# Linear attention and a routed feed-forward: rows of h scattered by expert slot, statistics and gates per unit

## Chip, cores and metric

One core of one Trainium2 chip. The metric is the device time of one execution in microseconds (us); lower is better. Five engines run their own instruction streams and meet at semaphores: TensorE (PE in the profile; its weight loads are PEld), VectorE (DVE), ScalarE (ACT), GpSimd (POOL) and SyncE (SP), which here only issues transfers.

## The reference, cut to what matters

```python
def _A_ref(x, wqkv, w_phi, wo):              # S = 2048 rows, D = 512, 32 heads of 16
    q, k, v = ...
    pq = jnp.einsum("bhsd,hdf->bhsf", q, w_phi)
    pk = jnp.einsum("bhsd,hdf->bhsf", k, w_phi)
    phi_q = jnp.concatenate([_softmax(pq, axis=-1), _softmax(-pq, axis=-1)], axis=-1)
    phi_k = jnp.concatenate([_softmax(pk, axis=-1), _softmax(-pk, axis=-1)], axis=-1)
    kv = jnp.einsum("bhsf,bhsd->bhfd", phi_k, v)
    z  = jnp.einsum("bhsf->bhf", phi_k)
    num = jnp.einsum("bhqf,bhfd->bhqd", phi_q, kv)
    den = jnp.einsum("bhqf,bhf->bhq", phi_q, z)[..., None] + 1e-6
    return (num / den) ... @ wo

def _B_ref(x, w_gate, w1, w2):               # E = 8 experts, F = 1792, one expert a row
    logits = xf @ w_gate
    topk_idx = jnp.argsort(-logits, axis=-1)[:, :K]
    topk_val = jnp.take_along_axis(logits, topk_idx, axis=-1)
    gates = _softmax(topk_val, axis=-1)
    for e in range(E):
        w = (gates * (topk_idx == e)).sum(-1, keepdims=True)
        out = out + w * (_silu(xf @ w1[e]) @ w2[e])

h = x + _A_ref(_layernorm(x), ...)
h2 = h + _B_ref(_layernorm(h), ...)
```

Each row goes to the one expert with the largest logit. Everything is float32; the large products are computed as three products of a rounded high part and the remainder (`mm3`, lines 74 to 77).

## The kernel before, in words

The 2048 rows are 16 chunks of 128. The work has three stages.

**Features (lines 384 to 452).** For each chunk c the loop at line 409 loads x two chunks ahead on SyncE's queue (`s_ln`, `load_x`), normalises, transposes (`s_tr`), projects to k, v and q, and sums k-features times v over all chunks (`s_kv`, line 372). x has three buffers, its normalised form another three.

**Output and routing (lines 457 to 599).** For each chunk: numerator and denominator (`s_num`), transposes (`s_ot`), the output projection `po` (`s_wo`). `s_wo` adds x to make h, and computes h's mean and reciprocal deviation (bn_stats and aggregate on VectorE, two operations on GpSimd). h, these two and the gate are one row of 516 numbers in `hb`; two chunks are a batch, and `s_top` picks the expert of each row, computes the gate by powers on GpSimd, and sends the batch to a DRAM buffer `hbuf` in token order. `s_rank` counts each row's place within its expert by matmuls with triangular and all-ones matrices, and `s_inv` adds one-hot products into a table `ivf` that maps places to tokens. After eight chunks `s_star` takes the expert with the most rows so far as the first one; its weights `raw` are loaded, and `split_chunk` divides them into `whi` (ScalarE) and `wlo` (VectorE or, for 10 of the 16 quarter chunks, GpSimd), while the last chunks are still worked on. `s_first` gathers the first unit's rows; all four chunks of its gemm1 are computed in this stage, interleaved with the last output projections.

**Units (lines 601 to 807).** A unit is a block of 128 rows of one expert. `gather(u)` brings its rows from `hbuf` by an indirect transfer on GpSimd's queue, two units ahead. `prework` normalises and transposes them; `gemm1` (48 matmuls) goes through silu and transposes (`tr`, giving `hThi`, `hTlo`) to `gemm2` (`g2`, 42 matmuls into `my`), then `yo` is scattered to the output. Where the next unit has another expert, `split` divides new weights under a condition read from a table, chunks 4 to 6 in the unit itself and 0 to 3 in the unit before, and `fetch` loads the expert after it. ScalarE, VectorE and GpSimd all take part in these conditions. `tables` (line 639) computes the block tables inside unit 0, behind its transposes, and `index` turns places into token numbers with 22 comparisons against `ivf`.

The order of instructions on an engine is not the source order: the framework orders by readiness in its own estimate and by source position, so a later instruction whose inputs and buffers are there can be issued ahead. `issue_after` pins one behind another.

Of the kernel before, what the change touches and what calls it, by code (L numbers as in the profile page):

```python
# [21 lines left out]
P = 128  # L22
# [10 lines left out]
ROW = D + 4  # L33
# [8 lines left out]
def kernel(  # L42
# [17 lines left out]
    hbuf = dram.tile([S, ROW], F32, name="hbuf")  # L60
# [13 lines left out]
    def mm3(ps, ahi, alo, bhi, blo, first, last):  # L74
# [12 lines left out]
    iota128 = consts.tile([P, P], F32, name="iota128")  # L87
    G.iota(iota128, pattern=[[1, P]], base=0, channel_multiplier=0, allow_small_or_imprecise_dtypes=True)
    iotaS = consts.tile([P, NT], F32, name="iotaS")
    G.iota(iotaS, pattern=[[P, NT]], base=0, channel_multiplier=0, allow_small_or_imprecise_dtypes=True)  # L90
    tok1 = consts.tile([P, NT], F32, name="tok1")
    G.iota(tok1, pattern=[[P, NT]], base=1, channel_multiplier=1, allow_small_or_imprecise_dtypes=True)
# [11 lines left out]
                    pattern=[[1, EV], [-1, EV]], channel_multiplier=0)  # L104
    gidx = consts.tile([P, NU], I32, name="gidx")
    sidx = consts.tile([P, NU], I32, name="sidx")
    isnew = consts.tile([P, NU], I32, name="isnew")
# [3 lines left out]
    ivf = consts.tile([P, P], F32, name="ivf")  # L111
    cnt = consts.tile([P, E], F32, name="cnt")
    col = consts.tile([P, NU], F32, name="col")
    star = consts.tile([P, E], F32, name="star")
    est = consts.tile([P, 1], F32, name="est")
    esti = consts.tile([P, 1], I32, name="esti")
    ps = ctx.enter_context(tc.tile_pool(name="ps", bufs=4, space=PSUM))
# [19 lines left out]

    def gather(u):
        G.indirect_dma_start(out=xg[u % 3], out_offset=None, in_=hbuf if u else hbuf[0:S // 2, :],
                             in_offset=bass.IndirectOffsetOnAxis(ap=gidx[:, u:u + 1], axis=0))  # L140

    def prework(u):
        g = xg[u % 3]
        xi = V.tensor_scalar(xn2[0], g[:, 0:D], g[:, D:D + 1], g[:, D + 1:D + 2], op0=OP.subtract, op1=OP.mult)
        pt = bank("mtr")
        for k in range(KD):
            T.transpose(pt[:, k * P:(k + 1) * P], xn2[0][:, k * P:(k + 1) * P], ident)
        ptv = pt.rearrange("p (k t) -> p k t", k=KD)
        hi_of(xhi[u % 2], ptv)
        lo_of(xlo[u % 2], ptv, xhi[u % 2])  # L150
        return xi
# [16 lines left out]
    LO = (V,) * NW  # L168

    def split_chunk(c, lo=None, n=2):  # L170
        for i in range(n):
            w = slice(i * (CW // n), (i + 1) * (CW // n))
            hi_of(whi[c][:, w], raw[c][:, w])
            eng = lo or LO[c]
            eng = eng[i] if isinstance(eng, tuple) else eng
            eng.tensor_tensor(wlo[c][:, w], raw[c][:, w], whi[c][:, w].bitcast(F32), op=OP.subtract)  # L176
# [15 lines left out]
    with ExitStack() as actx:  # L192
# [11 lines left out]
        csg = keep.tile([P, 2, E // 2], F32, name="csg")  # L204
        xwg = keep.tile([P, NT, 2, E // 2], F32, name="xwg")
        kvbd = keep.tile([P, NG, 68], F32, name="kvbd")
        V.memset(kvbd, 0.0)
        cum = [keep.tile([P, E], BF16, name=f"cum{c}") for c in range(NT + 1)]
        V.memset(cum[0], 0.0)
        V.memset(ivf, 0.0)  # L210
# [50 lines left out]
        def s_num(c):  # L261
            load_x(c)
            o = row("o", 2, "pc").rearrange("p (h f) -> p h f", f=DH)
            for i in range(2):
# [6 lines left out]
                V.tensor_scalar(den, nv[:, :, DH:DH + 1], 1e-6, None, op0=OP.add)  # L271
                V.reciprocal(den, den)
# [9 lines left out]
        if True:  # L282
            wp = c1.enter_context(tc.tile_pool(name="wp", bufs=1))
            wgs = wp.tile([P, KD, E], F32, name="wgs")
            onesf = wp.tile([P, P], F32, name="onesf")
# [74 lines left out]
            def s_v(c):  # L360
# [4 lines left out]
                mc = work.tile([P, 2, E // 2], F32, name="mc")  # L365
                G.tensor_scalar(mc, csg, st[c]["mv"][:, 0:1], None, op0=OP.mult)
                G.tensor_tensor(xwg[:, c], xwg[:, c], mc, op=OP.add)
# [33 lines left out]
            V.tensor_copy(csg.rearrange("p i e -> p (i e)"), pc[:, 0:E])  # L401
# [4 lines left out]
            def s_q(c):  # L406
                st[c]["tq"] = feat1(proj(st[c]["x"], wqhi, wqlo, "pq"))

            for c in range(NT - 1):
# [7 lines left out]
                if c == 3:  # L417
                    pg = bank("pog")
                    for dt in range(KD):
                        for t in range(4):  # L420
                            T.matmul(pg[:, dt * E:(dt + 1) * E], woT_raw[t // 2][:, t % 2, dt * P:(dt + 1) * P],
                                     wgs[:, t, :], start=(t == 0), stop=(t == 3))
# [21 lines left out]
            for i in range(2):  # L444
                for h in range(4):
                    V.tensor_copy(kvbd[32 * h:32 * h + 32, 4 * i:4 * i + 4, 17 * h:17 * h + 17],
                                  kvps[i][32 * h:32 * h + 32, :, 17 * h:17 * h + 17])
# [9 lines left out]
        def s_wo(c):  # L457
            b, j = divmod(c, NB)
            po = proj2(st[c]["oT"], wohi, wolo, "po")
            if j == 0:  # L460
                bt[b]["hb"] = work.tile([P, NB * ROW], F32, name="hb", tag="ph", bufs=3).rearrange(
                    "p (j r) -> p j r", r=ROW)
                G.memset(bt[b]["hb"][:, :, D + 3:D + 4], 0.0)
                bt[b]["lg"] = work.tile([P, NB, E], F32, name="lg", bufs=3)
            h = bt[b]["hb"][:, j, :]
            V.tensor_tensor(h[:, 0:D].rearrange("p (i d) -> p i d", i=2), po[:, :, 0:D // 2],
# [3 lines left out]
            ln_rstd(h[:, 0:D], h[:, D:D + 2], h[:, D + 1:D + 2])  # L470
            V.scalar_tensor_tensor(lg, csg, h[:, D:D + 1], lg, op0=OP.mult, op1=OP.subtract)

        def s_top(b):
            hb, lg = bt[b]["hb"], bt[b]["lg"]
            mn = work.tile([P, NB, 1], F32, name="tmn")
            V.tensor_reduce(mn, lg, AX.X, OP.min)
            eq = work.tile([P, NB, E], F32, name="eq")
            V.tensor_tensor(eq, lg, mn.to_broadcast([P, NB, E]), op=OP.is_equal)
# [9 lines left out]
            gt = work.tile([P, 3, NB, 1], F32, name="gt")  # L488
            nr = work.tile([P, NB, 1], F32, name="nr")
            V.tensor_reduce(gt[:, 0], mn, AX.X, OP.min)  # L490
            G.tensor_tensor(gt[:, 0], gt[:, 0], mn, op=OP.subtract)
            G.tensor_tensor(gt[:, 0], gt[:, 0], hb[:, :, D + 1:D + 2], op=OP.mult)
            G.tensor_tensor(gt[:, 1], euler.to_broadcast([P, NB]).unsqueeze(2), gt[:, 0], op=OP.pow)
            G.tensor_scalar(gt[:, 2], gt[:, 1], 0.0, None, op0=OP.add)
            G.tensor_tensor(nr, gt[:, 2], mone.to_broadcast([P, NB]).unsqueeze(2), op=OP.pow)
            G.tensor_tensor(hb[:, :, D + 2:D + 3], gt[:, 1], nr, op=OP.mult)
            nc.sync.dma_start(hbuf[b * NB * P:(b + 1) * NB * P, :].rearrange("(c p) r -> p c r", p=P), hb)

        def s_rank(b):
# [8 lines left out]
            rk = work.tile([P, NB], F32, name="rk")  # L508
            V.tensor_reduce(rk, rs, AX.X, OP.add)
            bs = work.tile([P, NB], F32, name="rb")  # L510
            V.tensor_scalar(bs, rk, 0.25 - P / 2, FLOOR, op0=OP.add, op1=OP.add)
            V.tensor_scalar(bs, bs, FLOOR, None, op0=OP.subtract)
            sl = work.tile([P, NB], F32, name="sl")
            V.tensor_tensor(sl, rk, bs, op=OP.subtract)
            am = work.tile([P, NB, P], F16, name="am")
            bm = work.tile([P, NB, E, NT], F16, name="bm")
            for j in range(NB):
                c = b * NB + j
                V.tensor_scalar(am[:, j, :], iota128, sl[:, j:j + 1], None, op0=OP.is_equal)
                jm = work.tile([P, NT], F16, name="jm")  # L520
                V.tensor_scalar(jm, iotaS, bs[:, j:j + 1], tok1[:, c:c + 1], op0=OP.is_equal, op1=OP.mult)
                V.tensor_tensor(bm[:, j], bc(oh[:, j, :], NT), mid(jm, E), op=OP.mult)
# [331 lines left out]
```

## Time and profile before

| | |
|---|---|
| median of 3 runs (lowest to highest) | 733.07 us (732.66 to 734.25) |
| profiled execution, its own time | 732.92 us |
| its span | 731.2 us |
| TensorE busy, mean granted clock | 702.0 us (96%), 0.987 |
| VectorE, ScalarE, GpSimd busy | 468.8, 303.2, 180.8 us |
| features, output and routing, units | about 0 to 205, 205 to 317, 317 to 731 us |
| bytes moved | 87.61 MB, 9.21 MB of it written |

In rows of groups, `out<-in` names what is written and read, then shapes, the count, the busy time and the mean of one in ns, then the idle time of the engine just before and what ended it. In the timeline, a row has start and duration, and in brackets the idle time before it with the releaser. A DMA-issue row shows the issuing only.

### The profile page before, as it was taken

The numbers are of one execution on the slowest core, as the hardware profiler recorded it, in microseconds if no ns is written. First come the engines' busy times: TensorE is split into PE (matmuls) and PEld (weight loads), VectorE is DVE, ScalarE is ACT, GpSimd is POOL, SyncE is SP. The second block draws the span as 40 slices with busy tenths as digits, with TensorE's granted clock in tenths as the row PEclk, the third lists the DMA queues.
The fourth block names the chain that finished last, engine by engine and source line by source line (L and its number), as shares of the span: only waits on it lengthen the run. The fifth ranks groups of instructions, "written<-read, shape, count | busy, mean of one in ns | idle before, by whom it ended". The sixth has DMA issues, their size and how long they took to land.

```text
span 731.2 us, 12523 instructions
## 1 busy us (share of the span) xinstructions
PE 702.0 (96%) x4130; PEld 612.2 (84%) x4130; DVE 468.8 (64%) x969; ACT 303.2 (41%) x458; POOL 180.8 (25%) x281
## 2 busy tenths in 40 slices
PE   6999999999999998779999999999999999999996
PEld 6899999999989997658888888888888878888885
DVE  4996987878787889794512999972185472922211
ACT  4534444434322015152112888862274463822211
POOL 3364645434313328521110011110011111011110
PEclk9999999999999999899999999999999999999999
DMA  9111101100002249417400799981066381001000
GB/s 332 57 30 44 30 15 30 30 15 1 1 16 73 74 156 341 153 34 294 193 29 2 258 369 376 344 345 53 30 210 241 121 328 31 11 29 30 30 30 6
DMA packets 21912, 87.61 MB, mean 120 GB/s; under 512 B 3070, under 2 KB 3582, under 8 KB 14656
## 3 DMA queue, kind: packets, MB, share of 16 engines
q1 hardware_dynamic: 18624, 76.86, 28.8%
q0 software_dynamic: 3200, 9.75, 4.0%
q8 instruction: 34, 0.56, 0.3%
q14 instruction: 54, 0.44, 0.2%
HBM read 78.18 MB, written 9.21 MB: 120 GB/s over the span
## 4 chain that ended last, share of the span: by engine, by line
issue 46%; PE 35%; DMA 10%; DVE 6%; POOL 1%; ACT 1%; POOLq 1%; SPq 0%; DVEq 0%
DMA out_dram<-yo,sidx 8%; PE kvps L372 4%; PE pn L267 3%; PE pq L75 2%; PE pq L77 2%; PE pq L76 2%; PE ptq L381 2%; PE pv L77 2%; PE pv L76 2%; PE pv L75 2%; PE pk L75 2%; PE pk L77 2%; PE pk L76 2%; PE po L75 2%; PE po L76 2%
## 5 line engine op out<-in xcount | busy, mean ns | idle before, releaser
L69 ACT ACTIVATE whi<-raw 128x1024 fp32r<-128x1024 f32 (+1 forms) x120 | 118.7, 1003 | 67.9 <-PE mh L77 37.4
L176 DVE TENSOR_TENSOR wlo<-raw,whi 128x1024 fp32r<-128x1024 f32 (+1 forms) x110 | 130.6, 1200 | 18.6 <-ACT whi L69 12.5
L75 PE MATMUL mh<-whi,xhi 128*128 128x512 f32 (+1 forms) x304 | 114.9, 378 | 0.0
L77 PE MATMUL mh<-whi,xlo 128*128 128x512 f32 (+1 forms) x304 | 111.5, 367 | 0.0
L76 PE MATMUL mh<-wlo,xhi 128*128 128x512 f32 (+1 forms) x304 | 111.4, 366 | 0.0
L798 POOL DMA_INDIRECT out_dram<-yo,sidx x19 | 21.5, 1131 | 352.5 <-DVEq L635 202.0
L76 PE MATMUL my<-wlo,hThi 128*128 128x512 f32 x266 | 104.7, 393 | 3.5 <-DVE wlo L176 3.3
L75 PE MATMUL my<-whi,hThi 128*128 128x512 f32 x266 | 106.0, 399 | 0.3 <-ACT hThi L69 0.3
L77 PE MATMUL my<-whi,hTlo 128*128 128x512 f32 x266 | 104.6, 393 | 0.3 <-DVE hTlo L72 0.3
L72 DVE TENSOR_TENSOR hTlo<-mtr,hThi 128x512 fp32r<-128x512 f32 x76 | 47.0, 621 | 86.2 <-ACTq L635 53.3
L163 ACT ACTIVATE hs<-mh 128x512 f32<-128x512 f32 x76 | 41.0, 540 | 145.3 <-PE mh L77 145.3
L355 POOL TENSOR_TENSOR ph<-t,sm 128x1024 f32<-128x1024 f32 x32 | 62.1, 1939 | 66.9 <-DVE sm L353 37.8
L77 PEld LDWEIGHTS mh<-whi,xlo 128*128 128x128 f32 x304 | 57.2, 188 | 10.2
L76 PEld LDWEIGHTS mh<-wlo,xhi 128*128 128x128 f32 x304 | 57.3, 189 | 9.3
L75 PEld LDWEIGHTS mh<-whi,xhi 128*128 128x128 f32 x304 | 57.2, 188 | 9.3
L797 DVE SCALAR_TENSOR_TENSOR yo<-my,xg 128x512 f32<-128x512 f32 x19 | 14.2, 748 | 78.4 <-PE my L77 78.4
L76 PEld LDWEIGHTS my<-wlo,hThi 128*128 128x128 f32 x266 | 50.3, 189 | 14.2 <-DVE wlo L176 4.3
L77 PEld LDWEIGHTS my<-whi,hTlo 128*128 128x128 f32 x266 | 50.3, 189 | 11.2 <-DVE hTlo L72 0.5
L75 PEld LDWEIGHTS my<-whi,hThi 128*128 128x128 f32 x266 | 50.4, 189 | 10.5 <-ACT hThi L69 0.5
L352 DVE TENSOR_REDUCE sm<-t 128x64 f32<-128x1024 f32 x32 | 38.8, 1214 | 12.0 <-ACT t L347 11.9
L727 PE MATMUL mtr<-ident,hs 128*128 128x128 f32 x266 | 41.7, 274 | 2.7 <-DVE hTlo L72 2.6
L347 ACT ACTIVATE t<-t 128x1024 f32<-128x1024 f32 x32 | 33.9, 1061 | 20.9 <-DVE t L346 19.8
(206 smaller groups left out, 1407.3 us busy)
## 6 DMA issues: line engine op xcount, KB each, us to landing
raw<-in_w_dram SPq DMA_DIRECT2D x56, 1024.0 KB, 5.2
xt<-in_x_dram SPq DMA_DIRECT2D x32, 256.0 KB, 2.7
hbuf<-hb SPq DMA_DIRECT2D x8, 516.0 KB, 3.8
phT<-in_wqkT_dram SPq DMA_DIRECT2D x4, 512.0 KB, 5.1
phT<-in_wv_dram SPq DMA_DIRECT2D x2, 512.0 KB, 6.4
phT<-in_wo_dram SPq DMA_DIRECT2D x2, 512.0 KB, 8.2
phT<-in_woT_dram SPq DMA_DIRECT2D x2, 512.0 KB, 5.6
xg<-hbuf,gidx POOLq DMA_INDIRECT x21, 3.7
```

The source lines that it names most:

```text
L69: A.activation(dst, src, AF.Copy)
L72: V.tensor_tensor(dst, src, hi.bitcast(F32), op=OP.subtract)
L75: T.matmul(ps, ahi, bhi, start=first, stop=False)
L76: T.matmul(ps, ahi, blo, start=False, stop=False)
L77: T.matmul(ps, alo, bhi, start=False, stop=last)
L163: A.activation(hs[c % 2][:, 0:fw], p[:, 0:fw], AF.Silu)
L176: eng.tensor_tensor(wlo[c][:, w], raw[c][:, w], whi[c][:, w].bitcast(F32), op=OP.subtract)
L347: A.activation(t, t, AF.Exp)
L352: V.tensor_reduce(sm, t, AX.X, OP.add)
L355: G.tensor_tensor(ph.rearrange("p (a f) -> p a f", f=DH), t, bc(sm, DH), op=OP.mult)
L372: T.matmul(kvps[g // 4][:, g % 4, :], ph[:, g * P:(g + 1) * P], vt[:, 4 * g:4 * g + 4, :].rearrange("p h f -> p (h f)"), start=(c == 0 and ...
L727: T.transpose(pt[:, j * P:(j + 1) * P], hs[c % 2][:, j * P:(j + 1) * P], ident)
```

## The change

- `hbuf` has 8 x 2048 rows of 514 numbers: h, the largest logit, the token number. Each expert owns 2048 rows. `cum[0]` starts at 16 per partition and expert so that `s_rank`'s sum is the row's slot itself; `s_rank` then sends each chunk by an indirect scatter from GpSimd (`send`), 16 in all, in place of 8 plain stores on SyncE's queue. It moves to the head of the loop's iteration.
- Rows that no token fills must hold a token number that the output scatter drops, so `s_blank` writes one blank row to all of `hbuf`, in 14 transfers on SyncE's queue, one for each iteration of the feature loop.
- The one-hot products, `s_inv`, `ivf` and `index` go. A unit's row numbers are now base plus partition.
- Mean, deviation and gate are computed per unit, from the gathered rows (`stats`, `gating`). In `s_wo` the statistics go; the mean is removed from the logits by centred gate weights `wgc`, which also removes GpSimd's correction in `s_v`.
- The 1e-6 of the denominator is added once, in `kvbd`.
- All splits of the first expert's weights are on VectorE, two quarter chunks an iteration from c = 12; none is on GpSimd. GpSimd no longer takes part in the conditions.
- Of unit 0 one chunk of gemm1 is computed ahead of the tables, three behind them. `tables1` (row numbers) comes first in unit 0, with gathers 1 and 2 behind it; `tables2` (flags) comes after `tr(2)`. In later units `stats(u + 1)` stands behind the split of chunk 4, and `prework(u + 1)` behind `g2(0, 2)` and `tr(3)`.

```diff
-ROW = D + 4
+ROW = D + 2
-    hbuf = dram.tile([S, ROW], F32, name="hbuf")
+    hbuf = dram.tile([E * S, ROW], F32, name="hbuf")
...
+    def send(c, rows, hrow):
+        i = G.indirect_dma_start(out=hbuf, out_offset=bass.IndirectOffsetOnAxis(ap=rows, axis=0),
+                                 in_=hrow, in_offset=None)
+        for other in sent + fetched:
+            tc.declare_no_dep(i.ins, other.ins, reason="other rows of hbuf")
+        sent.append(i)
+
     def gather(u):
...
+        i = G.indirect_dma_start(out=xg[u % 3], out_offset=None, in_=hbuf,
+                                 in_offset=bass.IndirectOffsetOnAxis(ap=gidx[:, u:u + 1], axis=0))
+        for other in sent:
+            tc.add_manual_dep(i.ins, other.ins.name, mybir.DependencyInfo(
+                mybir.DependencyClass.Sync, mybir.DependencyReason.DATA), reason="rows of hbuf")
+        fetched.append(i)
+
+    def stats(u):
+        g = xg[u % 3]
+        bs = small.tile([P, 6], F32, name="ubs")
+        V.bn_stats(bs, g[:, 0:D])
+        V.bn_aggr(norm[:, u, :], bs)
+        ve = small.tile([P, 1], F32, name="uve")
+        G.tensor_scalar(ve, norm[:, u, 1:2], EPS, None, op0=OP.add)
+        G.tensor_tensor(norm[:, u, 1:2], ve, nhalf, op=OP.pow)
+        V.tensor_scalar(xn2[0], g[:, 0:D], norm[:, u, 0:1], norm[:, u, 1:2], op0=OP.subtract, op1=OP.mult)
+
+    def gating(u):
+        g = xg[u % 3]
+        sc = small.tile([P, 5], F32, name="usc")
+        V.tensor_reduce(sc[:, 0:1], g[:, D:D + 1], AX.X, OP.max)
+        G.tensor_copy(sidx[:, u:u + 1], g[:, D + 1:D + 2])
...
+        G.tensor_tensor(gate[:, u:u + 1], sc[:, 3:4], sc[:, 4:5], op=OP.mult)
...
     def prework(u):
-        g = xg[u % 3]
-        xi = V.tensor_scalar(xn2[0], g[:, 0:D], g[:, D:D + 1], g[:, D + 1:D + 2], op0=OP.subtract, op1=OP.mult)
         pt = bank("mtr")
...
-            eng.tensor_tensor(wlo[c][:, w], raw[c][:, w], whi[c][:, w].bitcast(F32), op=OP.subtract)
+            lo_of(wlo[c][:, w], raw[c][:, w], whi[c][:, w])
...
+            def s_blank(c):
+                n = E * S // (NT - 2) // P
+                lo, hi = c * n * P, min((c + 1) * n * P, E * S) if c < NT - 3 else E * S
+                n = (hi - lo) // P
+                nc.sync.dma_start(hbuf[lo:hi, :].rearrange("(p r) f -> p r f", p=P),
+                                  blank.to_broadcast([P, n, ROW]))
...
                 if c + 2 < NT:
                     s_ln(c + 2)
+                    s_blank(c)
...
-            ln_rstd(h[:, 0:D], h[:, D:D + 2], h[:, D + 1:D + 2])
-            V.scalar_tensor_tensor(lg, csg, h[:, D:D + 1], lg, op0=OP.mult, op1=OP.subtract)
...
-            nc.sync.dma_start(hbuf[b * NB * P:(b + 1) * NB * P, :].rearrange("(c p) r -> p c r", p=P), hb)
...
+            to = work.tile([P, NB], F32, name="to")
+            V.tensor_reduce(to, rs, AX.X, OP.add)
+            toi = slots[:, b * NB:(b + 1) * NB]
+            V.tensor_copy(toi, to)
+            G.tensor_copy(bt[b]["hb"][:, :, D + 1], tok[:, b * NB:(b + 1) * NB])
             for j in range(NB):
-                c = b * NB + j
-                V.tensor_scalar(am[:, j, :], iota128, sl[:, j:j + 1], None, op0=OP.is_equal)
-                jm = work.tile([P, NT], F16, name="jm")
-                V.tensor_scalar(jm, iotaS, bs[:, j:j + 1], tok1[:, c:c + 1], op0=OP.is_equal, op1=OP.mult)
-                V.tensor_tensor(bm[:, j], bc(oh[:, j, :], NT), mid(jm, E), op=OP.mult)
...
+                send(b * NB + j, toi[:, j:j + 1], bt[b]["hb"][:, j, :])
...
-        for c in range(NT + 8):
+        for c in range(NT + 2):
+            b, j = divmod(c - 3, NB)
+            if j == 0:
+                at(s_rank, b - 1, NT // NB)
...
-            if NT - 4 <= c < NT:
-                split_chunk(c - NT + 4, ((G, G, V, V), (G, G, G, V), (G, G, G, V), (G, G, V, V))[c - NT + 4], 4)
...
+            if c == NT + 1:
+                s_top(NT // NB - 1)
+            if NT - 4 <= c < NT + 2:
+                split_pieces(2)
+            if c == NT:
+                with tc.issue_after(st[NT - 3]["add"].ins):
+                    stats(0)
+            if c == NT + 1:
                 prework(0)
...
+        pre.append(gemm1(0, 0))
+        s_rank(NT // NB - 1)
+        split_pieces(len(pieces))
...
-                                                        engines=[ENG.Activation, ENG.DVE, ENG.Pool])
+                                                        engines=[ENG.Activation, ENG.DVE])
...
+        if u == 0:
+            tables1()
+            gather(1)
+            gather(2)
         g1(0)
         if u:
             split(u, 4)
+            if u + 1 < NU:
+                stats(u + 1)
+        else:
+            split_chunk(4)
         g1(1)
+        gating(u)
         tr(0)
         if u:
             split(u, 5)
+        else:
+            stats(1)
         g1(2)
         tr(1)
...
+            g2(py, 0, 4)
+            tr(3)
+            with tc.issue_after(held["gidx"].ins):
+                tables2()
...
+            g2(py, 4, 11)
+            prework(1)
+            g2(py, 11, 14)
...
+            g2(py, 0, 2)
+            tr(3)
+            if u + 1 < NU:
                 prework(u + 1)
```

More of the change, by code (lines that the diff above doesn't have):

```diff
@@ L719, in unit @@
+        V.tensor_tensor(le, mid(end, NU), bc(eend, EV), op=OP.is_le)
+        nx = rt.tile([P, NU], F32, name="nx")
+        V.tensor_reduce(nx, le, AX.X, OP.add)
+        V.tensor_scalar(nxt, nx, 1.0, float(E - 1), op0=OP.subtract, op1=OP.min)
+        V.scalar_tensor_tensor(more, nx, float(EV), nw, op0=OP.is_lt, op1=OP.mult)
     def unit(u):
@@ L755, in unit @@
             split(u, 6)
+        else:
+            split_chunk(5)
         g1(3)
```

244 lines of the change are left out of this document (91 added, 153 removed).

## Prediction

> **What bounds the kernel now.** I read the busy table and the 40 slices first, then ten-us windows, then the timeline inside the windows that stand out.
>
> ```profile
> PE 702.0 (96%) x4130; PEld 612.2 (84%) x4130; DVE 468.8 (64%) x969; ACT 303.2 (41%) x458; POOL 180.8 (25%) x281
> ```
>
> TensorE is busy for 702.0 of 731.2 us, so only its holes and its slow stretches can be won, unless its work shrinks. The windows (busy time of PE, PEld, DVE, ACT, POOL, then granted clock, DMA share, GB/s) show where they lie:
>
> ```profile
> 260.00:270.00 10.00, 10.00 (x94) 9.95 (x93) 7.82 (x42) 1.19 (x2) 3.10 (x8) 1.00 0.32 100
> 270.00:280.00 10.00, 8.03 (x71) 7.57 (x71) 8.22 (x39) 4.29 (x8) 4.92 (x9) 1.00 0.88 318
> 280.00:290.00 10.00, 8.80 (x55) 7.89 (x56) 10.00 (x30) 5.49 (x11) 9.58 (x13) 0.83 0.87 305
> 290.00:300.00 10.00, 5.56 (x37) 5.25 (x36) 10.00 (x34) 0.77 (x2) 9.07 (x15) 0.77 0.43 172
> 300.00:310.00 10.00, 10.00 (x65) 9.05 (x65) 5.65 (x25) 2.37 (x3) 3.19 (x8) 0.89 0.60 212
> 310.00:320.00 10.00, 9.67 (x59) 7.38 (x58) 8.86 (x45) 4.22 (x8) 3.23 (x8) 1.00 0.15 55
> 320.00:330.00 10.00, 6.26 (x24) 4.37 (x25) 9.76 (x34) 5.51 (x7) 2.16 (x2) 0.97 0.09 26
> 330.00:340.00 10.00, 10.00 (x41) 7.94 (x41) 6.08 (x16) 1.20 (x2) 2.00 (x2) 0.86 0.66 211
> ```
>
> From 260 to 270 us TensorE is full. Then it idles 1.97 + 1.20 + 4.44 us up to 300 and 0.33 + 3.74 us from 310 to 330, in sum 11.7 us. Its clock adds a loss: busy time times the missing share of the clock is 1.5, 1.3 and 1.1 us from 280 to 310 and 0.2 + 1.4 us from 320 to 340, in sum 5.5 us. So 17.2 us are lost between 270 and 340. VectorE is busy for all of 280 to 300, so it is what TensorE waits for. The timeline there:
>
> ```profile
> 279.93 0.77 PE L237 MATMUL pto<-ident,o 128*128 128x128 f32 x4 [1.97 <-DVE xl L72]
> 282.00:283.00 1.00, 1.00 (x7) 1.00 (x7) 1.00 (x10) 1.00 (x3) 0.83 (x3) 0.50 0.89 370
> 283.56 3.80 POOL L176 TENSOR_TENSOR wlo<-raw,whi 128x512 fp32r<-128x512 f32 x3
> 283.67 1.31 DVE L519 TENSOR_SCALAR am<-iota,sl 128x128 f16<-128x128 f32 x1
> 294.97 0.17 PE L504 MATMUL pl<-oh,tri 128*128 128x8 bf16 x1 [2.51 <-DVE oh L483]
> 328.55 0.50 PE L76 MATMUL my<-wlo,hThi 128*128 128x512 f32 x1 [3.33 <-DVE wlo L176]
> ```
>
> A VectorE instruction that takes 0.34 us on average (L519 below) takes 1.31 us beside a GpSimd subtraction, and a hole of 1.97 us is followed by half clock. The second hole ends with the weight split of unit 0, which queues behind the tables.
>
> **The change part by part.** Two terms gain, two cost.
>
> *The scheduling stage, 270 to 340.* By-form groups (busy us, mean ns):
>
> ```profile
> L222 DVE BATCH_NORM_STATS2 bs<-hb 128x6 f32<-128x512 f32 x16 | 11.1, 694 | 0.0
> L471 DVE SCALAR_TENSOR_TENSOR lg<-csg,hb,lg 128x8 f32<-128x8 f32 x16 | 4.9, 306 | 0.0
> L519 DVE TENSOR_SCALAR am<-iota,sl 128x128 f16<-128x128 f32 x16 | 5.5, 342 | 0.0
> L521 DVE TENSOR_SCALAR jm<-iotaS,rb,tok 128x16 f16<-128x16 f32 x16 | 5.6, 348 | 0.0
> L522 DVE TENSOR_TENSOR bm<-oh,jm 128x128 f16<-128x128 bf16 x16 | 5.2, 328 | 0.0
> L271 DVE TENSOR_SCALAR den<-pn 128x16 f32<-128x16 f32 x32 | 5.2, 162 | 1.6 <-PE pn L267 1.4
> L176 POOL TENSOR_TENSOR wlo<-raw,whi 128x512 fp32r<-128x512 f32 x10 | 13.0, 1328 | 1.5 <-ACT whi L69 1.5
> L176 DVE TENSOR_TENSOR wlo<-raw,whi 128x512 fp32r<-128x512 f32 x6 | 4.6, 782 | 1.8 <-ACT whi L69 1.8
> L528 PE MATMUL acc<-bm,am 128*128 128x128 f16 x16 | 3.4, 226 | 0.4 <-DVE bm L522 0.4
> ```
>
> VectorE loses these six groups, 37.5 us over the 16 chunks, or 2.3 us a chunk. It takes over the 10 quarter-splits from GpSimd, 7.8 us at 782 ns. Some six chunks fall behind 270: 13.8 us leave, 7.8 enter, and the blocked stretches as at 283.67 lose their cause. Before, VectorE was busy for 28.2 of the 30 us from 270 to 300; the net 6 us and the blocked parts bring that near 20, while TensorE needs 30 less 7.6 idle less 2.8 of clock, 19.6. So the two are about level, and I leave 3 us of the 11.5 (7.6 idle, 3.9 clock) lost: **8.5 us** gained. The 16 `acc` matmuls go; their 226 ns overlap with neighbours, so between 0 and 3.4 us, and I take 0.7.
>
> In unit 0 the tables were computed before the hole's split; now three of the four gemm1 chunks (each chunk of 512 is 12 matmuls) stand beside tables and gathers, and the index inversion is gone. I take **4.2 of the 5.7 us** there. What can be late next is the chain last rank, two scatters, gather 1, statistics 1. From its rows:
>
> ```profile
> L798 POOL DMA_INDIRECT out_dram<-yo,sidx x19 | 21.5, 1131 | 352.5 <-DVEq L635 202.0
> xg<-hbuf,gidx POOLq DMA_INDIRECT x21, 3.7
> 424.41 0.74 DVE L797 SCALAR_TENSOR_TENSOR yo<-my,xg 128x512 f32<-128x512 f32 x1
> 446.32 0.74 DVE L797 SCALAR_TENSOR_TENSOR yo<-my,xg 128x512 f32<-128x512 f32 x1
> ```
>
> Two scatters of 1.1, about 3.7 to land (the gathers' figure), a gather of 1.1 and 3.7, statistics about 2: 13 us behind the rank. From one `yo` to the next a unit takes 21.9 us for 90 matmuls and 18 transposes. Behind the rank and ahead of prework(1) stand 36 matmuls of gemm1, 33 of gemm2 and the transposes, about 17 us of that. So the chain is hidden with 4 us to spare; without that cover it would cost its 13 us.
>
> All other edits of the stage (the centred gate weights, the epsilon in `kvbd`, the maximum in place of the minimum, POOL's mean correction) remove or move operations of 0.1 to 0.3 us on engines that wait there for TensorE, and I price them at nothing: the cover is the full TensorE of the 260 row. Without it they would be a gain still. The rank matmuls now stand at the head of an iteration, before `s_num`; if they are queued before the one-hot is there, 294.97 shows what it costs, 2.51 us, and there are seven: bound 0 to 17.6, taken 0, since the 260 row shows no wait with equally tight neighbours.
>
> *The units.* Each gets `stats` and `gating`: on VectorE bn_stats 0.69, aggregate and a 128x1 maximum at about 0.15 each (nearest: the small groups), so 1.0 us, and then the normalising instruction waits for two GpSimd results. In a split unit:
>
> ```profile
> 425.07 5.02 DVE L176 TENSOR_TENSOR wlo<-raw,whi 128x1024 fp32r<-128x1024 f32 x4
> 438.52 7.88 DVE L176 TENSOR_TENSOR wlo<-raw,whi 128x1024 fp32r<-128x1024 f32 x6
> 364.32 0.69 DVE L72 TENSOR_TENSOR hTlo<-mtr,hThi 128x512 fp32r<-128x512 f32 x1 [6.02 <-ACTq L635]
> L176 DVE TENSOR_TENSOR wlo<-raw,whi 128x1024 fp32r<-128x1024 f32 x104 | 126.0, 1224 | 16.8 <-ACT whi L69 10.7
> L226 POOL TENSOR_TENSOR hb<-ve,nhalf 128x1 f32<-128x1 f32 x16 | 9.5, 596 | 1.2
> ```
>
> In a unit without new weights VectorE waits 6 us at a time (364.32), so the additions are free. The 104 half-splits are 6 of unit 0 and 7 x 14, hence seven split units. The unit from 424.41 to 446.32 is one; 4 + 6 of its 14 half-splits stand above, with VectorE busy in them throughout. There +1.0 us and a wait of about 1.0 (two GpSimd operations, the power at 0.60, and the hand-over; an estimate) stand in the way of `hTlo` and of the splits behind it, on which TensorE waits. The last six half-splits are paced at 1.31 us against 1.22 of their own, so part is absorbed. Per split unit 0 to 2.0 us, seven times: 0 to 14, and I take **5**, nearer the lower end because three of the seven are followed by a unit with slack. GpSimd leaving the branches frees only GpSimd.
>
> *The fills.* New are 14 transfers from one blank row, 16384 x 514 x 4 bytes = 33.7 MB, through the queue that brings x. A full queue moved 318 GB/s at a share of 0.88 (270 row), 361; the 2 KB rows of x and h 100 at 0.32 (260 row), 312. That is 93 to 108 us in all, 6.7 to 7.7 for one. TensorE needs none of it, but x loads queue behind:
>
> ```profile
> 13.11 0.94 SPq L218 DMA_DIRECT2D xt<-in_x_dram  x2
> 17.62 0.33 SPq L218 DMA_DIRECT2D xt<-in_x_dram  x1
> 28.91 0.33 SPq L218 DMA_DIRECT2D xt<-in_x_dram  x1
> 33.67 0.44 PE pt L237 x4
> 36.87 1.74 PE kvps L372 x16
> 73.06 0.44 PE pt L237 x4
> SPq L300 <- DMA phT<-in_wqkT_dram: 0.7, 1, 0.7
> ```
>
> The load at 28.91 is chunk 5 (two at the start, two at 13.11, one at 17.62). The transposes at 33.67, before the first `kvps`, are chunk 2's, so 73.06 is chunk 5's: 44 us in hand. One fill an iteration costs nothing. The last row, a weight load waiting for the landing of one eight before it, without a common tile, suggests that no more than eight are under way. Bounds 0 and the 52 us of the rival below; I take **3**, for a few fills too many ahead of one load.
>
> Sum, on the profiled execution's own 732.9 us (span 731.2; the median of the runs is 733.1, 0.2 above): 732.9 - 8.5 - 0.7 - 4.2 + 5 + 3 = **727.5**.
>
> **The rivals.** *The fills run ahead (slower).* A fill waits for nothing, and the trace shows x loads issued 40 us ahead of use wherever a buffer is free. If all 14 enter the queue between 17.62 and 28.91, chunk 5 lands at 14 + 93 to 108 = 107 to 122 where 70 is needed: 37 to 52 us, or 727.5 - 3 + 45 = 769. It decides once some eight fills (56 us over 7) stand ahead of chunk 5. Against it: the eight under way.
>
> *VectorE bounds the split units.* 2.0 us in each of seven, 14 in place of 5: 736.5. If each wait of 2 us also drops the clock as at 279.93 (three us at half, 1.6 lost), 11 more: 747.
> The Trainium skill, "TensorE: Matmul & The Clock Gate", section "Why this matters for your kernels", asks only that gaps stay below about 3 us; by it the 747 is excluded. This trace disagrees: the 1.97 us gap came before half clock, so I keep the case.
>
> *The scatters and gathers are late.* If each of the three GpSimd DMAs of the chain is held as long as a run of four splits (5.02 in place of 1.1), 11.8 us come on top, less 4 spare: 7.8 later than forecast, 735.3.
> The Trainium skill, "SBUF — State Buffer", section "SBUF: two separate sides", says that GpSimd cannot write descriptors while VectorE holds the shared port; by its example, 620 ns growing to 3100, they would take five times as long, an estimate of 13 us more for three. The 1131 ns mean, measured beside such splits too, speaks against it.
>
> *Everything is hidden.* All 17.2 us won, units and fills 0 to 2: about 717. *The rank matmuls stall* at the head of an iteration, 1.2 us on average times seven: 736.
>
> **How the numbers follow.** Forecast 0.43 (719 to 731.4); fills ahead 0.15; VectorE bound 0.15; scatters late 0.12; all hidden 0.10; rank stalls 0.05. The range 715 to 748 leaves out the fills rival and little else, under 0.2. About 0.2%, 1.5 us, is what measurement tells from no change: faster is the forecast, the hidden case and a few shares of the late scatters, 0.54; the same 0.06; slower 0.40.
>
> **What would show it.** 270 to 340 right: no VectorE instruction of 1.3 us beside GpSimd, clock 1.00, no hole near 320. Units: 22 to 24 us from one `yo` to the next where weights are split, with a GpSimd releaser before the normalising row. Fills: DMA share near 1 in the first 120 us and any `bs` (L222) wait on x. It is wrong if TensorE stands between 70 and 120 us, or if a hole of some us stays before unit 1.

## The result, and the profile after

The changed kernel takes 767.08 us (median, 765.78 to 772.12), the kernel before 733.66 us in the same comparison: a ratio of 1.0459, with an interval of 1.0398 to 1.052. It is slower. The forecast was 727.5 us, its range 715 to 748, so the forecast is wrong in sign and in size. The profiled execution of the changed kernel took 772.12 us, the highest of the four, with a span of 770.3 us. What follows compares that span with the 731.2 us of the kernel before.

First the engines' busy times of the changed kernel:

```profile
PE 708.8 (92%) x4114; PEld 616.4 (80%) x4114; DVE 449.9 (58%) x824; ACT 304.6 (40%) x458; POOL 224.3 (29%) x353
```

TensorE has 16 matmuls fewer and is busy 6.8 us longer, so part of its work runs slower; its idle time grows from 29.2 to 61.5 us. VectorE has become less busy, not more. Where the time went shows best between one `yo` and the next, from the start times in the trace (`yo` is the VectorE instruction that ends a unit; in us: the start of the first `yo`, the lengths of some of the units 1 to 18, and the sum over all 18):

| kernel | first `yo` | unit 1 | units 2, 3 | unit 4 | unit 5 | unit 6 | unit 7 | unit 8 | unit 11 | units 1 to 18 |
|---|---|---|---|---|---|---|---|---|---|---|
| before | 336.2 | 21.4 | 21.3, 21.4 | 24.2 | 21.9 | 21.9 | 21.9 | 19.1 | 19.1 | 388.2 |
| after | 337.4 | 30.3 | 21.4, 21.4 | 24.0 | 31.0 | 28.7 | 27.6 | 19.9 | 22.8 | 424.6 |

The stage ahead of the first `yo` costs 1.2 us more, the units 36.4, the stretch from the last `yo` start to the end 1.5 (770.3 - 762.0 against 731.2 - 724.4). Five units, 1, 5, 6, 7 and 11, hold 34.2 of the 36.4. The windows of the changed kernel (length, then busy time of PE, PEld, DVE, ACT, POOL, granted clock, DMA share, GB/s), first those that answer to the windows of before, then unit 1 and a stretch of unit 5:

```profile
260.00:270.00 10.00, 10.00 (x93) 9.95 (x92) 6.89 (x33) 1.15 (x2) 2.11 (x3) 1.00 0.52 143
270.00:280.00 10.00, 4.67 (x44) 4.38 (x42) 1.62 (x7) 5.66 (x11) 0.99 (x1) 0.89 0.99 402
280.00:290.00 10.00, 6.15 (x36) 6.18 (x37) 5.46 (x17) 0.00 (x0) 3.06 (x5) 0.59 0.56 194
290.00:300.00 10.00, 9.78 (x86) 9.44 (x85) 8.24 (x29) 5.02 (x10) 0.86 (x2) 1.00 0.68 242
300.00:310.00 10.00, 7.73 (x59) 7.16 (x60) 8.99 (x29) 1.80 (x3) 6.18 (x11) 1.00 0.19 76
340.00:350.00 10.00, 6.93 (x40) 5.74 (x39) 0.00 (x0) 2.56 (x5) 3.73 (x8) 0.98 1.01 420
350.00:360.00 10.00, 5.96 (x20) 5.08 (x21) 4.23 (x9) 1.58 (x3) 2.87 (x9) 0.51 0.43 179
440.00:450.00 10.00, 3.41 (x23) 3.00 (x23) 4.64 (x7) 3.02 (x5) 3.88 (x7) 0.76 0.30 111
```

Before, TensorE idled here beside a full VectorE. Now it idles beside an idle one: VectorE is busy for 1.62 of ten us from 270 to 280 and for nothing at all from 340 to 350. Both stand. The timeline says for what. Rows of VectorE, GpSimd's DMA issues, SyncE's issues and TensorE, in the stage and in unit 1; the bracket at a row's end is the idle time of its engine before it, and what ended it:

```profile
271.52 0.36 DVE L531 TENSOR_TENSOR cum<-cum,oh 128x8 bf16<-128x8 bf16 x2
282.26 0.15 DVE L174 TENSOR_REDUCE usc<-xg 128x1 f32<-128x1 f32 x1 [10.39 <-DMA xg<-hbuf,gidx]
282.34 0.69 DVE L72 TENSOR_TENSOR wlo<-raw,whi 128x512 fp32r<-128x512 f32 x1
282.95 0.68 DVE L511 TENSOR_TENSOR hb<-po,xt 128x512 f32<-128x512 f32 x1
265.55 2.00 SPq L223 DMA_DIRECT2D raw<-in_w_dram  x4
276.49 0.99 POOL L154 DMA_INDIRECT xg<-hbuf,gidx  x1 [8.26 <-DMA hbuf<-hb,slots]
283.85 0.56 PE L75 MATMUL po<-wohi,xh 128*128 128x260 f32 x1 [9.18 <-DVE lg L515]
...
333.87 5.95 SPq L656 DMA_DIRECT2D raw<-in_w_dram  x7
343.83 0.98 POOL L154 DMA_INDIRECT xg<-hbuf,gidx  x1 [0.30 <-issue]
352.24 0.69 DVE L164 BATCH_NORM_STATS2 ubs<-xg 128x6 f32<-128x512 f32 x1 [12.80 <-DMA xg<-hbuf,gidx]
354.04 1.09 PE L736 MATMUL mtr<-ident,hs 128*128 128x128 f32 x4 [7.11 <-DVEq L659]
```

At 271.9 VectorE reaches the maximum of `gating(0)`, which reads the gathered rows of unit 0. In the source it stands in unit 0, behind `tables1`; in the program VectorE reaches it some 45 us before `tables1` is done (317.0). The gather it reads has not even been issued: it waits on GpSimd's queue until the two scatters ahead of it have landed, and it lands at 282.2. Everything behind the maximum in VectorE's queue waits too: the weight split at 282.34 and the `hb` add at 282.95 follow without a wait of their own (no bracket), and TensorE's next matmul needs the bank that this add and the `lg` add behind it read. In unit 1 the `bn_stats` that waits for 12.80 us is that of unit 3, which the source has in unit 2. The gather for it was issued at 343.83. VectorE's waits of this kind, in us in total, their number and the longest; then the gathers in the changed kernel (21 issues, ns min/median/max, and the time to landing), and the time to landing in the kernel before:

```profile
DVE ubs L164 <- DMA xg<-hbuf,gidx: 75.2, 15, 12.8
DVE usc L174 <- DMA xg<-hbuf,gidx: 10.4, 1, 10.4
DVE xn L169 <- POOL norm L168: 8.9, 6, 2.3
```

```profile
L154 POOL DMA_INDIRECT xg<-hbuf,gidx x21: 956/979/997, 276.5 to 743.1; - x21
DMA to landing us min/median/max: 3.3/3.4/8.4
```

```profile
DMA to landing us min/median/max: 3.3/3.7/8.5
```

The gathers themselves are no later than before (8.4 against 8.5 at most). They are late where seven weight loads of 1 MB are in the queues ahead of them (SyncE's row at 333.87, a DMA share of 1.01). What is new is that VectorE asks for their rows at once. In units 2 to 4 `bn_stats` starts 3.4 us after the gather's issue and the units are no longer than before; in units 1, 5, 6, 7 and 11 it starts 8.4, 7.6, 6.6, 5.6 and 5.9 us after it, and these are the units that grew.

### The profile page after: what moved, and what is told of

Its sections match the earlier page's. It is cut to its first block, busy times and chain, and to the rows that moved or that the text cites. A ratio compares the mean times of both kernels' runs of the same rounds, so it can differ in the third digit from the quotient of the medians.

```text
span 770.3 us, 12259 instructions
## 1 busy us (share of the span) xinstructions
PE 708.8 (92%) x4114; PEld 616.4 (80%) x4114; DVE 449.9 (58%) x824; ACT 304.6 (40%) x458; POOL 224.3 (29%) x353
## 5 line engine op out<-in xcount | busy, mean ns | idle before, releaser
L72 DVE TENSOR_TENSOR wlo<-raw,whi 128x1024 fp32r<-128x1024 f32 (+1 forms) x120 | 134.4, 1151 | 13.1 <-ACT whi L69 8.9
L75 PE MATMUL my<-whi,hThi 128*128 128x512 f32 x266 | 110.4, 415 | 0.0
L76 PE MATMUL my<-wlo,hThi 128*128 128x512 f32 x266 | 107.0, 402 | 1.2 <-DVE wlo L72 1.2
L77 PE MATMUL my<-whi,hTlo 128*128 128x512 f32 x266 | 106.6, 401 | 1.4 <-DVE hTlo L72 1.3
L810 POOL DMA_INDIRECT out_dram<-yo,sidx x19 | 23.5, 1235 | 240.3 <-DVEq L659 138.0
L736 PE MATMUL mtr<-ident,hs 128*128 128x128 f32 x266 | 44.3, 286 | 27.3 <-DVE hTlo L72 16.9
L736 PEld LDWEIGHTS mtr<-ident,hs 128*128 128x128 f32 x266 | 34.3, 147 | 37.2 <-issue 27.4
L75 PEld LDWEIGHTS my<-whi,hThi 128*128 128x128 f32 x266 | 52.0, 196 | 9.5
L164 DVE BATCH_NORM_STATS2 ubs<-xg 128x6 f32<-128x512 f32 x20 | 13.9, 694 | 77.8 <-DMA xg<-hbuf,gidx 75.2
L809 DVE SCALAR_TENSOR_TENSOR yo<-my,gate,xg 128x512 f32<-128x512 f32 x19 | 14.2, 749 | 76.4 <-PE my L77 69.2
```

The costliest lines, as they stand in the source:

```text
L72: V.tensor_tensor(dst, src, hi.bitcast(F32), op=OP.subtract)
L75: T.matmul(ps, ahi, bhi, start=first, stop=False)
L76: T.matmul(ps, ahi, blo, start=False, stop=False)
L77: T.matmul(ps, alo, bhi, start=False, stop=last)
L164: V.bn_stats(bs, g[:, 0:D])
L736: T.transpose(pt[:, j * P:(j + 1) * P], hs[c % 2][:, j * P:(j + 1) * P], ident)
```

## The experiments

The theory: the planner (the pass that puts each engine's instructions into their final order, which need not be that of the source) moved the two VectorE instructions that read gathered rows, `bn_stats` and the maximum, up to directly behind the gather, and VectorE, which takes its queue in order, stands there. The rivals: the fills (the forecast's own rival of 769 us comes to within 2 us of the measured time), the added statistics wherever they stand, and late gathers in any order. Each ratio below is against the kernel before, run beside it on the same chip. Differences in us between versions are mostly between medians of separate sessions, in which the kernel before took 733.15 to 734.65, so they are good to about 1 to 2 us.

**An order edge in the first stage.** `behind` adds an edge that fixes issue order alone; no work goes.

```
+    def behind(i, first):
+        if first is not None:
+            tc.add_manual_dep(i.ins, first.ins.name, ...NoSync...)
-        V.tensor_reduce(sc[:, 0:1], g[:, D:D + 1], AX.X, OP.max)
+        behind(V.tensor_reduce(sc[:, 0:1], g[:, D:D + 1], AX.X, OP.max), first)
-        gating(u)
+        gating(u, None if u else held["gidx"])
```

> The changed kernel with one order edge: the max copy of gating(0), which reads the rows of gather(0), is queued on VectorE behind the last instruction of tables1; no work is removed. Theory (VectorE stands at the head of its queue on rows that have not landed, 10.39 us at 282.26 in the profiled changed kernel): the hole at 272-282 goes, the 12.7 us that the forecast saw in 270-336 come back by 7 to 10 of them, so 757 to 760 us against 767. Rival (the fills and the rows' traffic set that time, the order only shows it): the wait moves to the bn_stats of unit 0 and the time stays at 765 to 769.

Measured: 762.95 us (759.25 to 766.13), ratio 1.04 (1.0361 to 1.0438). In its profile the hole of the stage is gone, with a smaller one left from 290 on:

```profile
270.00:280.00 10.00, 10.00 (x92) 9.95 (x91) 8.10 (x28) 6.08 (x11) 1.16 (x1) 1.00 0.98 393
280.00:290.00 10.00, 9.49 (x83) 9.19 (x82) 8.15 (x28) 5.57 (x11) 3.50 (x5) 1.00 1.03 414
290.00:300.00 10.00, 7.92 (x55) 7.59 (x53) 7.63 (x24) 0.00 (x0) 3.60 (x5) 0.83 0.35 135
```

The first `yo` starts at 328.2 in place of 337.4, 9.2 us earlier, and from the first `pn` (the matmul that opens the output stage) to it the run takes 119.5 us in place of 129.3. The median moved by 4.1 and misses the expected 757 to 760, and the two ranges overlap by a hair; units 1, 5, 6 and 7 are about as long as they were (28.3, 30.2, 30.0, 28.4).

**The order edges in the units.**

```
-        V.bn_stats(bs, g[:, 0:D])
+        behind(V.bn_stats(bs, g[:, 0:D]), first)
-                stats(u + 1)
+                stats(u + 1, held["y", u - 1])
-        gating(u)
+        gating(u, held["y", u - 1] if u else None)
```

> The changed kernel with order edges in the units alone: from unit 1 on, bn_stats of stats(u+1) and the max copy of gating(u) are queued on VectorE behind the y of unit u-1, so that they stand one unit after the gather that they read, as in the source; no work is removed. Theory (head-of-queue wait on a fresh gather, 12.8 us in unit 1 and about 7 us in units 5 to 7): units 1, 5, 6 and 7 fall from 27.6 to 31.0 us towards 22 to 24, in all 25 to 33 us less: 734 to 742 us. Rival A (the added statistics and their way over GpSimd cost the time wherever they stand): within 3 us of 767. Rival B (late gathers cost the time in any order): the normalise or the transposes wait instead, 760 us or more.

Measured: 746.26 us (742.08 to 749.31), ratio 1.0141 (1.0086 to 1.0195), 20.8 us less than the changed kernel, where 25 to 33 were expected. Unit 1 falls to 21.1 us, units 5 to 7 to 25.0, 24.2 and 25.9, and of the 15 waits of `bn_stats` one is left:

```profile
DVE ubs L169 <- DMA xg<-hbuf,gidx: 3.5, 1, 3.5
DVE usc L179 <- DMA xg<-hbuf,gidx: 10.6, 1, 10.6
```

The hole of the first stage stays, as its row shows. Rivals A and B fall: the same work and the same gathers, in another order, cost 26.2 us less in the units (398.4 against 424.6).

**Both.** 

> Both sets of order edges. Theory: the gains add, 724 to 735 us, so level with or below the 733.7 us of the kernel before. Rivals A and B of the run with the edges in the units: 755 us or more.

Measured: 736.44 us (732.17 to 738.61), ratio 1.0032 (1.0014 to 1.0049): 30.6 us less than the changed kernel, and still 2.2 above the kernel before, just outside the expected 724 to 735. The trace is of the fastest of the ten executions (732.17 us, span 730.4). In it the first `yo` starts at 325.4; the units sum to 396.7, 8.5 above before. Units 5 to 7 take 24.2, 24.2 and 25.0. VectorE's and GpSimd's rows behind the `y` of unit 6 show what is left:

```profile
463.30 0.18 DVE L170 BATCH_NORM_AGGREGATE norm<-ubs 128x2 f32<-128x6 f32 x1
466.36 0.55 DVE L174 TENSOR_SCALAR xn<-xg,norm 128x512 f32<-128x512 f32 x1 [2.88 <-POOL norm L173]
462.95 1.12 POOL L815 DMA_INDIRECT out_dram<-yo,sidx  x1 [15.62 <-DVE yo L814]
464.38 0.98 POOL L154 DMA_INDIRECT xg<-hbuf,gidx  x1 [0.30 <-issue]
465.74 0.58 POOL L173 TENSOR_TENSOR norm<-uve,nhalf 128x1 f32<-128x1 f32 x1
```

The aggregate ends at 463.48. GpSimd issues a scatter and a gather before it turns to the power, and the normalise waits 2.88 us for it with the weight splits queued behind.

**One read of fresh rows in the kernel before.** The test in the other direction: nothing of the change but one VectorE instruction more in a unit, put ahead of the unit's first `hTlo` (`c == 0`).

```
         if 0 < u < NU - 2:
             gather(u + 2)
+            peek = pk[u % 2]
+            held["peek"] = V.tensor_reduce(peek, xg[(u + 2) % 3][:, D:D + 1], AX.X, OP.max)
...
+            if c == 0 and 0 < u < NU - 2:
+                tc.add_manual_dep(i.ins, held["peek"].ins.name, ...NoSync...)
```

> The kernel before, with one VectorE instruction more in units 1 to 20: a max over one column (128x1, about 0.15 us) of the rows that the unit's own gather has just asked for, in the place where the changed kernel has bn_stats (behind the y of the unit before and one weight split, ahead of the first hTlo). Its value goes nowhere. Nothing else of the change is in it: no fills, scatters, unit statistics or moved splits. Theory (an instruction that reads a fresh gather holds VectorE's queue): unit 1 and units 5 to 7 grow as in the changed kernel, by about 9, 7, 7 and 6 us, so 752 to 764 us. Rival (it takes the change's traffic or its added work): 738 us or less (15 to 20 instructions of 0.15 us).

Measured: 764.57 us (763.81 to 765.33), ratio 1.0409 (1.0359 to 1.0459). A read of one column, 18 times 0.15 us, costs 29.9 us, nearly the whole loss of the change. Its waits in sum, its row in unit 1, and the window beside that:

```profile
DVE pk L725 <- DMA xg<-hbuf,gidx: 84.6, 18, 10.1
```

```profile
350.42 0.15 DVE L725 TENSOR_REDUCE pk<-xg 128x1 f32<-128x1 f32 x1 [10.15 <-DMA xg<-hbuf,gidx]
```

```profile
340.00:350.00 10.00, 10.00 (x54) 8.35 (x52) 0.27 (x1) 2.77 (x5) 1.99 (x2) 1.00 0.93 356
```

Units 5 to 7 take 29.7, 30.7 and 30.5 us in place of 21.9. Unit 1 does not follow the expectation: VectorE stands for 10.15 us there as well, but TensorE is full until 350.2 and the unit grows by 1.3 us, not by 9. The gather's issue tells why:

```profile
339.52 0.75 DVE L804 SCALAR_TENSOR_TENSOR yo<-my,xg 128x512 f32<-128x512 f32 x1 [0.62 <-PE my L77]
341.88 0.97 POOL L139 DMA_INDIRECT xg<-hbuf,gidx  x1 [0.30 <-issue]
```

Here the gather goes out 2.4 us behind the `yo`, and VectorE is free 10.9 us behind it. In the changed kernel GpSimd first works through two units' gates and one unit's deviation (337.14 to 341.77) and a scatter; the gather goes out 6.4 us behind the `yo` (343.83 against 337.39), and VectorE is free after 14.9 us. TensorE has work in hand for about ten us in both (10.7 and 9.5), so the one wait is nearly covered and the other is not. GpSimd's added work thus has a part in unit 1's loss.

**Fewer fill bytes.** 768 rows of `hbuf` for each expert in place of 2048, enough for these inputs (`room`, `base9`, `cum[0]`, the clip of `gidx` and `s_blank` follow the constant).

```
+C = 768
-    hbuf = dram.tile([E * S, ROW], F32, name="hbuf")
+    hbuf = dram.tile([E * C, ROW], F32, name="hbuf")
```

> The changed kernel with 768 rows of hbuf for each expert in place of 2048 (enough for these inputs), so 12.6 MB of fills in place of 33.7 MB; all else as it is. The forecast's rival (fills run ahead of the x loads) put the whole loss on them: 730 to 737 us. Theory (they cost the 2.8 us by which the first pn is later, 208.1 against 205.3): 764 to 766 us, and the wait at 272-282 stays.

Measured: 766.35 us (764.59 to 771.23), ratio 1.0453 (1.0403 to 1.0503), 0.7 us less than the changed kernel. The forecast's rival fell: it named nearly the right time for the wrong reason. The same edit on top of both order edges:

> Both sets of order edges, and 768 rows for each expert in place of 2048. With the other waits gone, theory: the fills' 2.8 us at the first pn come back whole or in part, 1 to 3 us less than 736.4. Rival (they cost nothing that shows): 735.5 to 737.5 us.

Measured: 728.38 us (726.93 to 731.91), ratio 0.9924 (0.9897 to 0.995), 8.1 us less than the order edges alone, more than the theory's 1 to 3.

**The statistics a unit earlier, on purpose.** `stats` is cut in two: `bn_stats`, aggregate and power of unit u+2 stand behind the third `hTlo` of unit u, the normalise (`rows`) alone behind the `y` of the unit before.

```
-                stats(u + 1, held["y", u - 1])
+                if u == 1:
+                    stats(2, held["y", 0])
+                rows(u + 1, held["y", u - 1])
...
         tr(2)
+        if 0 < u < NU - 2:
+            stats(u + 2, held["tr", 2])
```

> Both sets of order edges, and the statistics of unit u+2 taken late in unit u (bn_stats behind the third hTlo of the unit, about 13 us after the gather), the normalise alone left behind the y of the unit before. Theory: of the 8.5 us by which the units with the order edges are still longer than before (units 6 to 8: 24.2, 24.2, 25.1 against 21.9), the wait of the normalise for GpSimd's pow (2.9 us at 466.36, GpSimd issuing two transfers first) is the cause; it goes, 727 to 731 us. Rival (VectorE's added work of about 1 us in a unit that splits weights): 735 to 737 us.

(By the table's count those are units 5 to 7.) Measured: 727.87 us (724.43 to 730.99), ratio 0.9924 (0.9888 to 0.9961). The normalise's wait for the power falls to this, in the run with both order edges and in this one:

```profile
DVE xn L174 <- POOL norm L173: 53.6, 20, 5.0
```

```profile
DVE xn L177 <- POOL norm L173: 6.6, 3, 5.0
```

The trace is of the fastest of five executions. The units now sum to 388.2 us, the sum of the kernel before. Where the gain sits is hard to see from the `yo`, which VectorE can start late: by their starts units 5 to 7 still take 23.9, 23.4 and 24.0, and unit 8 takes 15.7 in place of 19.2. From the start of one unit's last gemm2 matmul to that of the next, units 5 to 7 take 21.9 each before, 24.2, 24.2 and 25.0 with both order edges, and 21.4, 23.0 and 23.3 here; unit 8 takes 21.4 in all three. So most of it sits where it was expected (5.7 of the 7.7 us by which these three were longer), and some 0.7 us more comes from each of the units 4, 10, 12 and 14 (22.0 to 22.1, now 21.4).

**Unit 0 as well.** `stats(1)` behind the second `hTlo` of unit 0.

```
-            stats(1)
+            stats(1, held["tr", 1])
```

> As the run with the statistics late in the unit before, and in unit 0 the bn_stats of stats(1) queued behind the second hTlo (VectorE stood 2.99 us ahead of it, and TensorE waited for the hTlo behind it). Theory: 1 to 3 us less than that run, 725 to 729 us, and faster than the kernel before. Rival (the chain from gather(1) to the rows of unit 1 is what ends unit 0): the same as that run.

Measured: 725.09 us (724.47 to 726.83), ratio 0.9869 (0.9833 to 0.9904). This version beats both kernels, the kernel before by 1.3%. Its advantage of 2.8 us over the run before it is of the expected size, but the intervals of the two overlap, and from the first `pn` to the first `yo` its trace gains only 0.9 us (116.5 against 117.4). So the gain over that run is not shown.

> The run with the statistics late in the unit before and those of unit 1 behind the second hTlo, with 768 rows for each expert in place of 2048. Theory: the fills cost some 4 to 8 us once no wait hides them (first pn at 202.8 against 206.7 and the time 8.1 us less, in the two runs with the order edges alone): 717 to 721 us. Rival (the 8.1 us of those two runs was the difference of single starts): 723 to 726 us.

Measured: 721.34 us (717.07 to 724.25), ratio 0.982 (0.9767 to 0.9873), 3.8 us less than with all 2048 rows, the intervals overlapping. Three pairs of runs thus give the 21 MB of fills 0.7, 8.1 and 3.8 us. The traces of the three pairs agree better: with fewer rows the first `pn` comes 4.7, 3.9 and 4.3 us earlier.

**The split move alone**, in the kernel before:

```
-                split_chunk(c - NT + 4, ((G, G, V, V), (G, G, G, V), (G, G, G, V), (G, G, V, V))[c - NT + 4], 4)
+                split_chunk(c - NT + 4, V, 4)
```

> The kernel before, with one part of the change alone: the ten quarter-splits of the first expert's weights that GpSimd has go to VectorE, in the same places; statistics, inversion, tables and stores as before. The forecast gave the whole stage 270 to 310 8.5 us, since 13.8 us of VectorE work leave and 7.8 enter. Theory: without the work that leaves, VectorE (busy for 28.2 of the 30 us there) only gets longer by up to 7.8 us less what the blocked stretches give back (13 us of GpSimd splits, in which a VectorE row of 0.34 us took 1.31): 731 to 738 us. Rival (GpSimd's hold on VectorE is the whole loss): 722 to 728 us.

Measured: 732.85 us (730.54 to 734.48), ratio 0.9993 (0.9976 to 1.001), no difference, as the theory had it. The holes only move:

```profile
270.00:280.00 10.00, 6.63 (x57) 6.01 (x55) 7.75 (x35) 4.29 (x8) 5.62 (x10) 1.00 0.92 338
280.00:290.00 10.00, 9.75 (x59) 9.70 (x59) 9.60 (x33) 5.54 (x11) 2.38 (x3) 0.66 1.01 402
290.00:300.00 10.00, 6.53 (x55) 6.02 (x53) 10.00 (x36) 0.60 (x1) 6.92 (x10) 1.00 0.41 131
```

VectorE is as full as before, 27.35 of 30 us against 28.2. Taking GpSimd off the splits pays nothing by itself. Whether removing the VectorE work alone would have paid was not run.

## Why the prediction was wrong

**The step that failed is the pricing of the units:** "In a unit without new weights VectorE waits 6 us at a time (364.32), so the additions are free", and "Per split unit 0 to 2.0 us". It counted how long the new instructions take and never asked what they read, how old that is, and where in VectorE's queue they would be put. It took their place from the source, where the rows are a unit old, though the planner is free to issue a ready instruction ahead. The program has `bn_stats` one unit earlier, behind a gather issued a moment ago. The term was +5 and came out at +36.4. Its bounds, 0 to 14, were too narrow for the same reason: they were bounds on durations. "Free" was wrong in kind, too: unit 1 splits no weights and lost 8.9 us, because VectorE stood for a gather that landed 8.4 us after its issue, while the weights for later units were loading.

**The mechanism that was priced held.** The wait of the normalise for GpSimd, which the forecast named as a sign to look for, is in the trace of the run with both order edges, 2.88 us behind the `y` of unit 6, and the units stand 8.5 us above before there, against the forecast's 5. In sum that cost vanishes once the statistics are taken earlier (388.2), though units 6 and 7 keep 1.1 and 1.4 us of it.

**The stage 270 to 340** was given 8.5 + 0.7 + 4.2 = 13.4 us. In the changed kernel the first `pn` is 2.8 us late (208.1 against 205.3) and the first `yo` 1.2, so 1.6 us were won between them. With both order edges the first `pn` comes at 206.7, 1.4 late, and the first `yo` 10.7 us early: 12.1 us won. So what the lighter VectorE work was to bring came nearly in full, and one misplaced maximum of 0.15 us hid most of it (9.2 us at the first `yo`, by the run with its edge alone). From 270 to 300 VectorE was busy for 24.0 us (8.12, 8.35 and 7.50 of ten), where the forecast said near 20, and in place of the 3 us that it left lost there 4.6 were: 3.4 of idle time (9.49 and 7.11 of ten us busy from 280 to 300) and 1.2 of clock. Of the forecast's two signs of being wrong one came true: a hole stayed ahead of unit 1.

**The chain rank, scatters, gather, statistics** was put ahead of unit 1 and found hidden with 4 us to spare. In the run with both order edges VectorE does wait 2.99 us for the gather of unit 1, and moving the `bn_stats` behind the second `hTlo` went with 2.8 at the medians, which is within their intervals. The same wait for scatters and gather also stands ahead of unit 0's gating, and there it was not priced: it is the 10.39 us at 282.26.

**"The scatters and gathers are late"** was the rival nearest in kind, at 735.3. It had lateness as a fixed delay on one chain, not as a delay that recurs in VectorE's queue in every unit that loads weights. The gathers' issues did not slow, 0.96 to 1.00 us in the row above; the landings did, where weight loads were under way. The Trainium skill, "SBUF — State Buffer", section "SBUF: two separate sides", which the forecast set against its row, is about the writing of descriptors, which the forecast took for a part of the issue, and no run here shows that it slowed.

**The fills** were given 3 us, "for a few fills too many ahead of one load", and that held: the mechanism is the one named, and the size is 2.8 to 4.7 us. In the changed kernel the first `pn` is 2.8 us late; in the six traces with all the fills it comes at 206.7 to 211.4, in the three with fewer rows at 202.8 to 206.7, against 205.3 before. SyncE's fill issues, the one window between 20 and 160 us in which TensorE is not full, and the rows that lead to its hole, all in the changed kernel:

```profile
L450 SPq DMA_DIRECT2D hbuf<-blank x14: 617/940/4417, 13.9 to 125.1; - x14
```

```profile
140.00:150.00 10.00, 8.69 (x55) 7.88 (x54) 7.38 (x12) 4.20 (x7) 3.14 (x5) 0.91 1.01 239
141.97 0.69 DVE L257 BATCH_NORM_STATS2 bs<-xt 128x6 f32<-128x512 f32 x1 [3.98 <-DMA xt<-in_x_dram]
145.60 1.93 POOL L392 TENSOR_TENSOR ph<-t,sm 128x1024 f32<-128x1024 f32 x1 [7.37 <-DVE sm L390]
147.59 1.44 PE L415 MATMUL ptq<-ident,ph 128*128 128x128 f32 x8 [1.31 <-POOL ph L392]
```

The fills are not all issued at once; one goes out behind each x load, until 125.1, so the rival of 769 us was wrong. But x lands in 8.9 us (median) in place of 2.7, VectorE stands 3.98 us at the head of its queue for an x load, the `ph` on GpSimd comes late behind it, and TensorE stands for 1.31 us. It is the change's main fault again, on a smaller scale. All six traces with all the fills have TensorE waiting for `ph` ahead of the first `pn`, for 1.3 to 4.0 us in all; the three with fewer rows have no such wait.

**The rank matmuls** were given nothing; in the run with both order edges TensorE waits for a one-hot once, 2.2 us.

## What to carry to other kernels

Before pricing an added instruction by its duration, ask when its operand is ready, and where the planner will put it: on an engine that takes its queue in order, the wait belongs to everything queued behind it. An engine that is idle for a third of its time does not make an addition free if the addition waits on something that is not there. When TensorE idles beside an engine that idles too, put an order edge on the instruction at the end of that engine's hole before undoing any of the work.

## What the runs showed of the hardware

Eighteen instructions of 0.15 us, each of which reads a transfer too early, cost 29.9 us together. VectorE stood for 84.6 us in them; the rest, about two thirds, did not show in the time, as in unit 1, where TensorE had work in hand. The Trainium skill, "PSUM — Partial Sum Buffer", section "Engine vs sequencer instructions", says that VectorE's queue is strictly first in, first out. The traces agree: the two rows behind the 10.39 us at 282.26 start in sequence, with no wait of their own.

A gather of 128 rows lands in 3.4 us (median), and in up to 8.4 us while weight loads run at 420 GB/s (window 340 to 350, share 1.01), with its issue unchanged at 0.98 us; no run took the weight loads away, so that they are the cause is read from the rows alone.

In the changed kernel's holes of 9.18 and 7.11 us in TensorE the granted clock falls to 0.50 some three us after the hole begins, and stays there for about ten us (278 to 288 and 350 to 360, by windows of one us). So 4.2 and 5.8 us of the matmuls behind the holes run at half clock, which costs a further 2.1 and 2.9 us. The hole of 1.31 us that ends at 147.59 is followed by some three us at half clock as well (0.60, 0.50, 0.50 and 0.70 in the four us from 148); in the run with both order edges holes of up to 1.8 us in the same stage are not.
